# DeltaNet and SwiGLU on one core: weights converted by thirds of columns, the norm's weight moved to x, and a new plan of the start

## The chip, the cores and the metric

The kernel runs on one core of one Trainium2 chip. The metric is the time of one execution in microseconds of device time; the times below are the median of three runs, and one further execution was profiled. Engines are named as in the profile: PE is TensorE (PEld its weight loads), DVE is VectorE, ACT is ScalarE, POOL is GpSimd, and SP issues most of the transfers.

## The reference

Attention first, with a state for each of 4 batches x 8 heads, then a feed-forward network over 3072 tokens. All is float32, except that the kernel gets the three weight matrices as float64 from the host and converts them on the chip.

```
for t in range(768):                                  # q, k, v: (4, 8, 768, 48)
    y[t]  = q[t] @ state                              # k_n = k / (|k| + 1e-6)
    v_old = state.T @ k_n[t]
    state = state + beta[t] * outer(k_n[t], v[t] - v_old)
x   = y as (3072 tokens, 384)
xn  = x / sqrt(mean(x*x) + 1e-6) * rms_g
out = (silu(xn @ w_gate) * (xn @ w_val)) @ w_out      # d_ff = 1536
```

## The kernel before

**Tiling.** The sequence is cut into 12 chunks of 64 steps (`NCH`), each for all 32 heads. Every chunk has the same stages:

- `load` fetches k, q and v. `norms` makes 1/|k|: a square on ACT (L558), a sum on DVE (`ksum`), a power on POOL (`knrm`, L562), then `krec` on DVE.
- `prep` scales k by `krec` (L628), turns it with PE (`turn`, L517), forms the scores k k^T (`scores`, L540), and solves a triangular system: the scores go through DRAM (`dkk`) into a layout by head (`at`, L656). A recursion of fifteen steps on DVE (`step`: L703 and L709) inverts two 32-step blocks at once. The result goes through DRAM again (`dx`) into `mt` and `x2bd`, and PE merges the blocks (L760, L784, L808). For chunks 0 and 1 ("early") DVE does the scaling of `at`; later POOL does.
- `qpart` makes the masked scores of q and k (`pt`, L580).
- `recur` applies the system to v minus the state's part (L895), multiplies with `pt` (L909), updates the state (L1022), takes the mean square (L949 for chunk 0, L961 later), its inverse root (`root`, L966 to L973, on POOL), scales y, and turns it into x for the feed-forward (L990 on PE, L993 copies on ACT).
- The feed-forward of chunks 0 and 1 is `ffn_plain` (L1067 up, L1049 down). From chunk 2 on it is `ffn`, with fewer products from sums of the weights that `factors` and `out_factors` prepare (L1160 up, L1216 down).

**Weights.** `weights` has 18 loads of 768 KB into three `raw` buffers. A load's float64 words become float32 by a Prelu on ACT (L456), two bit operations and one product on DVE (L444, L447, L452), and a sum. The sum is made by PE and ACT for the first three loads (L467, L468, L476), by DVE for the others (L484, L486). For gate and val one load is 128 rows by 768 columns, and the norm's weight g, one number for each row, is multiplied in during the conversion. The list `ready` holds what an up-matmul waits for: all three loads of its matrix and half.

**Order.** Every instruction group goes into the class `Plan` with its engine, an estimated duration and a due time. Plan lays all groups out in time, forward by start time and due time, backward for new due times, 60 rounds with random shakes from a fixed seed, and keeps the best order; this order is then issued, engine by engine. `PERIOD` spaces the due times of the chunks, `STICK` is what a change of PE's tiling mode is charged, `FETCH` and `AHEAD` describe how fast PE can get its instructions and how many it holds, and `after` is the time before which a transfer is not planned. In the planned gaps of PE before 70 us `filler` puts matmuls without a use (L1306). ACT issues some transfers of chunk 0 on a queue of its own; all others go through SP.

Of the kernel before, what the change touches and what calls it, by code (L numbers as in the profile page):

```python
# [18 lines left out]
W = 32  # L19
# [6 lines left out]
STICK = 2.0  # L26
# [23 lines left out]
def fillers(a, b):  # L50

    n, t = 0, max(a, 2.0)
    while t < b - 0.3:
        n, t = n + 1, t + (0.43 if t < 6.5 else 0.24)
    return n


class Plan:
# [47 lines left out]
    def forward(self, banks, until):  # L106
# [13 lines left out]
        while len(order) < len(self.ops):  # L120
            best = None
            for e in ENGINES:
                for op in cand[e]:
                    s = max(op.at, at[e])
                    if op.port:
                        s = max(s, held["POOL" if e == "DVE" else "DVE"])
                    n = sum(not g.taken for g in op.acquire)
                    if n > len(free):
                        continue
                    if n:  # L130
                        s = max(s, free[n - 1])
                    key = op.key + (STICK if op.mode is not None and op.mode != mode else 0.0)
                    if op.size and backlog + op.size - FETCH * op.dur > AHEAD:
                        key += 2.0 * STICK
                    if best is None or (s, key, op.n) < best[0]:
                        best = ((s, key, op.n), op)
# [13 lines left out]
            if op.eng == "PE":  # L150
                if s - at["PE"] > 1.4 and s > until:
                    end += 1.6
                backlog = max(0.0, backlog - FETCH * (s - at["PE"])) + op.size - FETCH * op.dur
                late = max(0.0, backlog - AHEAD) / FETCH
                backlog, end = max(0.0, backlog - FETCH * late), end + late
# [50 lines left out]
    def run(self, free, filler=None, until=0.0):  # L206
# [3 lines left out]
        rng = random.Random(1)  # L210
# [31 lines left out]
def kernel(  # L242
# [46 lines left out]
    g52 = sbt("g52", [128, KT])  # L289
# [72 lines left out]
    PERIOD = 50.5  # L362
# [42 lines left out]
    def load_small():  # L405
        for i in range(8):
            src = beta.rearrange("b (y g) (c i t) -> i g (b y) c t", i=2, g=2, t=W)[i // 2 % 2, i % 2]
            dma(beta_b[16 * i : 16 * i + 16], src, 0.5, w=[("beta", i)], work=0.2)
        dma(g_sb, moe_rms_g.rearrange("(t p) -> p t", p=128), 1, w=["g"], after=8.0)
        P.add("DVE", 0.1, lambda: nc.vector.tensor_scalar_mul(g52, g_sb, 2.0**-52), 30, r=["g"], w=["g52"])  # L410
# [6 lines left out]
    def weights():  # L417
        todo = []
        for half_ in range(2):
            c0 = half_ * WCOL  # L420
            for side, (key, w) in enumerate((("wg", moe_w_gate), ("wv", moe_w_val))):
                for t in range(KT):
                    src = w[t * 128 : t * 128 + 128, c0 : c0 + WCOL]
                    dst = w_in[:, side, half_, 3 * t : 3 * t + 3].rearrange("p i n -> p (i n)")
                    todo.append((dst, src, [(key, half_)], t))
            for f in range(6 * half_, 6 * half_ + 6, 2):
                src = moe_w_out[f * 128 : f * 128 + 256, :].rearrange("(a p) c -> p a c", a=2)
                z = spot(f)
                todo.append((wo_sb[:, z : z + 2].rearrange("p a c -> p (a c)"), src, [("wo", f), ("wo", f + 1)], None))
        for n, (dst, src, keys, gt) in enumerate(todo):  # L430

            gk = [] if gt is None else ["g", "g52"]
            pr = (30 if n < 9 else CV2) + 0.2 * n
            i, a = n % NRAW, n % NCV
            rdst = raw[i] if len(src.shape) == 2 else raw[i].rearrange("p (a c) -> p a c", a=2)
            dma(rdst, src, (0.1 if n == 0 else 3 + 2 * n), w=[("raw", i)], dur=0.7, work=3.06, after=(0.0, 5.0, 16.7, 24.5, 24.5)[n] if n < 5 else 50.0)
            words = raw[i].bitcast(U32).rearrange("p (n two) -> p n two", two=2)
            low, high = words[:, :, 0], words[:, :, 1]
            u = dst.bitcast(U32)
            cc = cvb[a]  # L440
# [10 lines left out]
            def s5(low=low, cc=cc, by=2.0**-52 if gt is None or n < NPE else g52[:, gt : gt + 1]):  # L451
# [7 lines left out]
            P.add("DVE", 1.0, s5, pr, r=[("raw", i)] + gk, w=cvk)  # L459
            done = []  # L460
            if n < NPE:
                for x_ in range(2):
                    ps = Group()
                    cols = slice(384 * x_, 384 * x_ + 384)

                    def s6(ps=ps, dst=dst[:, cols], cc=cc[:, cols]):
                        nc.tensor.matmul(ps.t[:, 0:384], ident, dst, start=True, stop=False)  # L467
                        nc.tensor.matmul(ps.t[:, 0:384], ident, cc, start=False, stop=True)  # L468

                    P.add("PE", 1.35, s6, pr, r=cvk + [("cvw", n), "ident"], w=[("cvp", n, x_)], ps=ps, size=8)  # L470
                    done.append(("cv", n, x_))
                    def s7(dst=dst[:, cols], ps=ps, gt=gt):
                        if gt is None:
                            nc.scalar.copy(dst, ps.t[:, 0:384])
                        else:
                            nc.scalar.mul(dst, ps.t[:, 0:384], g_sb[:, gt : gt + 1])  # L476

                    P.add("ACT", 0.48, s7, pr, r=[("cvp", n, x_), ("cvw", n)] + gk, w=[done[-1]], last=ps)
            else:
                done.append(("cv", n))  # L480

                def s8(dst=dst, cc=cc, gt=gt):
                    if gt is None:
                        nc.vector.tensor_tensor(out=dst, in0=dst, in1=cc, op=ALU.add)  # L484
                    else:
                        nc.vector.scalar_tensor_tensor(out=dst, in0=dst, scalar=g_sb[:, gt : gt + 1], in1=cc, op0=ALU.mult, op1=ALU.add)  # L486

                P.add("DVE", 0.97, s8, pr, r=cvk + gk, w=[("cvw", n), done[-1]])
# [6 lines left out]
    def load(c, what):  # L495
        t0 = c * C
        pk, pq, pv = ((-5, 1, 12), (5, 29, 36))[c] if c < 2 else (due(c, 150), due(c, 99), due(c, 70))
        for key, t, src, pr in (("k2", k2[c % NK], k, pk), ("q2", q2, q, pq)):
            for g in range(2):
# [4 lines left out]
                dma(dst, s, pr, w=[(key, c % NK if key == "k2" else 0, g)], dur=0.7, work=1.02, eng="ACT" if c == 0 and g and key == "k2" else "SP", after=((2.0, 0.0, 26.0), (6.0, 24.5, 34.0))[c]["kqv".index(key[0])] if c < 2 else 60.0)  # L504
        if "v" in what:
            for bb in range(2):
                s = v[2 * bb : 2 * bb + 2, :, t0 : t0 + C, :].rearrange("p h t e -> t (p h) e")
                dma(vt[64 * bb : 64 * bb + 64], s, pv, w=[("v", bb)], dur=0.85, work=1.02, after=(26.0, 34.0)[c] if c < 2 else 60.0)
# [61 lines left out]
    def qpart(c):  # L570
# [3 lines left out]
        turn(q2, qt, qk, [("q2", 0, 0), ("q2", 0, 1), "q2p"], pr, c == 0)  # L574
# [10 lines left out]
    def prep(c):  # L585
# [42 lines left out]
        P.add(e_, 1.1 if early else 1.6, lambda: eng.tensor_tensor(  # L628
            out=kd, in0=kd, in1=krec[i2][:, :, None].to_broadcast([128, 16, D]), op=ALU.mult,
        ), pr if early else pn, r=[("krec", i2)], w=kkeys)  # L630
        turn(kn, kt[ikq], ktk, kkeys + kp, pr, c == 0)
        ps = scores(kt[ikq], kt[ikq], pr, ktk, kkall)
        for d in range(2):
            dst = kk[ikk][:, :, d:16:2]
            src = lambda d=d, ps=ps: ps[d].t.rearrange("p (u i t) -> p i u t", u=8, i=2)
            if c or d == 0:
                P.add("ACT", A(512), lambda dst=dst, f=src: nc.scalar.mul(dst, f(), -1.0), pr, r=[ps[d]], w=kkd(d), last=ps[d])
            else:
                P.add("DVE", V(512), lambda dst=dst, f=src: nc.vector.tensor_scalar_mul(dst, f(), -1.0), pr, r=[ps[d]], w=kkd(d), last=ps[d])
# [55 lines left out]
        P.add(e_, 0.69 if early else 1.3, share1, pi, r=[("at", 0), ("at", 1)], w=xkeys)  # L695
# [35 lines left out]
        q_ = "SP" if c else "ACT"  # L731
        for par in range(2):
            dst = dx[i2].rearrange("i g x (s two) t -> two (i g x) s t", two=2)[par]
            dma(dst, x[64 * par : 64 * par + 64], pi, r=xkeys, w=[("dx", i2, par)], dur=0.63, work=1.0, eng=q_)
# [6 lines left out]
        for i in range(2):  # L741
            for bb in range(2):
                r0 = 64 * bb + W * i
                for g in range(2):
                    src = dx[i2][i, g, 8 * bb : 8 * bb + 8].rearrange("x s t -> s x t")
                    dma(mt[imt][r0 : r0 + W, 8 * g : 8 * g + 8, W * i : W * i + W], src, pi, r=xk, w=[("mt", imt, i, bb, g)])
        for y_ in range(4):
            src = dx[i2][1].rearrange("g (b y) s t -> y s (g b) t", y=4)[y_]
            dst = x2bd[W * y_ : W * y_ + W, :, y_]
            dma(dst, src, pi, r=xk, w=[("x2bd", y_)], eng=q_)  # L750
# [76 lines left out]
    def recur(c):  # L827
# [115 lines left out]
        for h in halves:  # L943
# [21 lines left out]

            def root(cols=cols):  # L966
                m = ms[i2][:, cols, 0]
                if c == 0:
                    nc.gpsimd.tensor_tensor(out=m, in0=m, in1=ms[i2][:, cols, 1], op=ALU.add)
                nc.gpsimd.tensor_scalar_add(m, m, 1e-6)  # L970
                nc.gpsimd.tensor_tensor(out=rs[i2][:, cols], in0=m, in1=mhalf[:, cols], op=ALU.pow)

            P.add("POOL", 1.1, root, py, r=["half"], w=[(k_, i2, p) for p in h for k_ in ("ms", "rs")])  # L973
# [11 lines left out]
            for p in h:  # L985
                psx = Group()

                def xtr(p=p, psx=psx):
# [4 lines left out]
                P.add("ACT", A(384), lambda p=p, psx=psx: nc.scalar.copy(  # L993
                    xdst[:, p:6:2], psx.t[:, 0:DM].rearrange("d (k t) -> d k t", k=KT)
                ), pxv, r=[psx], w=[xkeys[p]], last=psx)
# [15 lines left out]
        if c < NCH - 1:  # L1011
# [15 lines left out]
            for g in range(2):  # L1027
# [4 lines left out]
                else:  # L1032
                    P.add("DVE", V(384), lambda dst=dst, f=src: nc.vector.tensor_copy(out=dst, in_=f()), py + 3, r=[pss[g], ("xp", 0), ("xp", 1)], w=[("st", g)], last=pss[g])
# [22 lines left out]
    def ffn_plain(c, f0, f1, start):  # L1056
# [3 lines left out]
        def up(f):  # L1060
            ps = Group()
            h_, i_, n = f // 6, f % 6 // 2, 128 * (f % 2)
            for side, key in enumerate(("wg", "wv")):
# [8 lines left out]
                P.add("PE", 1.31, mm, start + 3.9 * (f - f0), r=xk + [("wuse", h_)] + ready[(key, h_)], w=[ps, (("sil", f % 2), ("hf", f, 0))[side]], ps=ps, size=12)  # L1072
# [40 lines left out]
    def factors(h):  # L1113
# [3 lines left out]
        wk = ready[("wg", h)] + ready[("wv", h)]  # L1117
# [80 lines left out]
    def down(c, start):  # L1198
# [12 lines left out]
        x, y, z_ = Group(), Group(), Group()  # L1211

# [28 lines left out]
        product(x, s2, s2k, wsum[:, 1], False, 4)  # L1241
        snap(u2, x, [("tmp", 0)])
# [9 lines left out]
        product(x, a(1, 1), ak(1, 1), wsum[:, 2], False, 12)  # L1252
        P.add("ACT", A(192), lambda: nc.scalar.copy(o_sb[1][:, 0:192], x.t[:, 0:192]), -1, r=[x], w=[("tmp", 4)], last=x)
# [86 lines left out]
```

## Time and profile before

| what | value |
|---|---|
| median of 3 runs (lowest to highest) | 721.37 us (721.09 to 725.16) |
| the profiled execution: time, span | 720.97 us, 718.9 us |
| busy share of the span: PE, PEld, DVE, ACT, POOL | 98%, 91%, 76%, 42%, 22% |
| first feed-forward matmul (L1067) | 75.43 us |
| fillers (L1306) | 320 records, 42.6 us |
| up-matmuls from chunk 2 on (L1160) | 2400 records, 305.4 us |
| moved by DMA | 54.68 MB, mean 76 GB/s |

The profile is of one execution. A matmul in float32 has two records. Matmuls are pipelined and their ends are modelled, so a busy PE is not PE at its peak. "issue" is time in which an engine waited for nothing that the profile shows. The chain of work that ended last is followed back from the last instruction, at each step to what released it, or to the instruction before it on its engine. A rate of the DMA over a stretch is the mean over all its queues.

### The profile page before, as it was taken

Reading aid. Unit: us, or ns where it says so; the run is one execution under the profiler, and the core shown is the slowest. Engines: PE = TensorE matmul, PEld = TensorE weight load, DVE = VectorE, ACT = ScalarE, POOL = GpSimd, SP = SyncE. Lnnn points to the kernel's source line nnn. Section 1 sums busy time; section 2 is a strip of 40 time slices with the busy share of each in tenths; the row PEclk is TensorE's granted clock in tenths of the full one; section 3 lists DMA queues with packets and bytes.
Section 4 is the critical chain, followed back from the end, with each engine's and each line's share of the span. In section 5 each row is a group of like instructions: output and inputs, shape, how many; then the busy total and the mean of one; then the engine's idle time right before and its main releaser. Section 6 shows DMA issues by size and latency. Waiting matters only on the chain.

```text
span 718.9 us, 23523 instructions
## 1 busy us (share of the span) xinstructions
PE 704.4 (98%) x10200; PEld 656.6 (91%) x10200; DVE 549.5 (76%) x1132; ACT 302.8 (42%) x679; POOL 155.3 (22%) x153
## 2 busy tenths in 40 slices
PE   8997998999999999999999999999999999999997
PEld 8796886877789999999999999999999999999997
DVE  5999789798979859829958959769669768648372
ACT  5423553324334535344435534445344445254240
POOL 4102207015132132122132132134032031000000
PEclk9999999999999999999999999999999999999999
DMA  8848688151262251351262352432521442100000
GB/s 184 217 73 219 174 205 232 21 96 25 46 118 47 35 108 25 56 107 25 45 121 46 48 95 47 79 64 46 90 53 26 79 64 38 24 18 2 23 1 23
DMA packets 206999, 54.68 MB, mean 76 GB/s; under 512 B 199216, under 2 KB 202288, under 8 KB 206896
## 3 DMA queue, kind: packets, MB, share of 16 engines
q1 hardware_dynamic: 201552, 52.19, 35.8%
q10 hardware_dynamic: 5344, 0.98, 0.8%
q8 instruction: 80, 1.31, 0.8%
q14 instruction: 23, 0.19, 0.1%
HBM read 40.83 MB, written 12.32 MB: 74 GB/s over the span
## 4 chain that ended last, share of the span: by engine, by line
PE 88%; DVE 7%; DMA 2%; issue 1%; SPq 1%; POOL 1%; ACT 0%; DVEq 0%; ACTq 0%
PE bank L1160 37%; PE bank L1216 19%; PE bank L1067 9%; PE bank L1049 4%; PE bank L849 3%; PE bank L540 3%; PE bank L517 2%; PE bank L895 2%; PE bank L808 2%; PE bank L909 2%; DVE acc L709 2%; PE bank L1022 1%; DVE acc L703 1%; PE bank L990 1%; PE bank L784 1%
## 5 line engine op out<-in xcount | busy, mean ns | idle before, releaser
L1160 PE MATMUL bank<-xf,w_in 128*128 128x128 f32 x1440 | 180.7, 277 | 0.0
L1170 DVE TENSOR_TENSOR tmp<-tmp,bank 128x512 f32<-128x512 f32 x180 | 121.4, 683 | 72.0 <-PE bank L1160 66.0
L1160 PEld LDWEIGHTS bank<-xf,w_in 128*128 128x128 f32 x1440 | 169.9, 192 | 2.4 <-issue 0.4
L1160 PE MATMUL bank<-xf,more 128*128 128x128 f32 x960 | 124.7, 277 | 0.0
L1160 PEld LDWEIGHTS bank<-xf,more 128*128 128x128 f32 x960 | 115.7, 192 | 1.7 <-issue 0.6
L1172 ACT COPY tmp<-bank 128x512 f32<-128x512 f32 x120 | 69.1, 586 | 73.2 <-PE bank L1160 56.9
L1176 ACT ACTIVATE tmp<-tmp 128x256 f32<-128x256 f32 x120 | 49.8, 418 | 100.0 <-DVE tmp L1170 99.9
L709 DVE TENSOR_REDUCE acc<-acc 128x30 f32<-128x90 f32 (+4 forms) x180 | 85.1, 473 | 6.2
L703 DVE TENSOR_TENSOR acc<-acc,at 128x60 f32<-128x60 f32 (+4 forms) x180 | 62.5, 347 | 5.2 <-POOL at L686 2.1
L1216 PE MATMUL bank<-wo_sb,hf 128*128 128x192 f32 x360 | 64.1, 328 | 0.2 <-DVE pt L580 0.2
L1216 PEld LDWEIGHTS bank<-wo_sb,hf 128*128 128x128 f32 x360 | 58.2, 190 | 0.7 <-DVE pt L580 0.4
L1177 DVE TENSOR_TENSOR hf<-tmp 128x256 f32<-128x256 f32 x120 | 52.9, 451 | 5.7 <-ACT tmp L1176 5.1
L562 POOL TENSOR_TENSOR knrm<-ksum,half 128x16 f32<-128x16 f32 x12 | 36.3, 3026 | 92.9 <-DVE ksum L561 87.8
L656 POOL TENSOR_TENSOR at<-at,beta_b 128x1024 f32<-128x1024 f32 x10 | 24.4, 2440 | 131.5 <-DMA at<-dkk 98.6
L1306 PE MATMUL bank<-ident 128*128 128x128 f32 x320 | 42.6, 294 | 1.4 <-POOL ident masks.py:199 1.4
L1306 PEld LDWEIGHTS bank<-ident 128*128 128x128 f32 x320 | 40.5, 207 | 2.4 <-POOL ident masks.py:199 1.4
L730 POOL COPY acc<-acc 128x128 f32<-128x128 f32 x40 | 21.1, 556 | 82.0 <-DVE acc L709 81.8
L1049 PE MATMUL bank<-wo_sb,hf 128*128 128x384 f32 x96 | 34.9, 492 | 0.0
L1225 DVE TENSOR_TENSOR tmp<-tmp,bank 128x192 f32<-128x192 f32 x30 | 10.6, 352 | 31.4 <-PE bank L1216 29.7
L1067 PE MATMUL bank<-xf,w_in 128*128 128x256 f32 x144 | 33.6, 384 | 0.0
L1067 PE MATMUL bank<-xp,w_in 128*128 128x256 f32 x144 | 33.5, 382 | 0.0
L1067 PEld LDWEIGHTS bank<-xf,w_in 128*128 128x128 f32 x144 | 27.1, 192 | 4.8 <-issue 0.4
(167 smaller groups left out, 1052.8 us busy)
## 6 DMA issues: line engine op xcount, KB each, us to landing
at<-dkk SPq DMA_DIRECT2D x23, 256.0 KB, 4.2
more<-in_moe_w_gate_dram SPq DMA_DIRECT2D x6, 768.0 KB, 4.7
q<-in_q_dram SPq DMA_DIRECT2D x24, 192.0 KB, 3.8
more<-in_moe_w_val_dram SPq DMA_DIRECT2D x6, 768.0 KB, 7.6
vt<-in_v_dram SPq DMA_DIRECT2D x24, 192.0 KB, 4.3
more<-in_moe_w_out_dram SPq DMA_DIRECT2D x6, 768.0 KB, 7.3
out_dram<-tmp SPq DMA_DIRECT2D x48, 96.0 KB, 2.2
k<-in_k_dram SPq DMA_DIRECT2D x23, 192.0 KB, 3.6
```

Of the source, the lines that this page charges most:

```text
L562: P.add("POOL", 2.95, lambda: nc.gpsimd.tensor_tensor(out=knrm[i2], in0=ksum[i2], in1=half, op=ALU.pow), pn, r=[("ksum", i2), "half"], w=[ ...
L703: nc.vector.tensor_tensor(out=acc[:, 1:3, 0:n, j + 2 : W].rearrange("p a i t -> p i a t"), in0=acc[:, old, 0:n, j : j + 2, None].to_broadc ...
L709: nc.vector.tensor_reduce(out=acc[:, new, 0:n, j + 2 : W], in_=acc[:, lo : lo + 3, 0:n, j + 2 : W].rearrange("p a i t -> p i t a"), axis=A ...
L1049: nc.tensor.matmul(po[p].t[:, 0:DM], hf[:, spot(f), 128 * p : 128 * p + 128], wo_sb[:, spot(f)], start=(f == f0), stop=(f == f1 - 1), skip ...
L1067: nc.tensor.matmul(ps.t[:, TOK * side : TOK * side + TOK], w_in[:, side, h_, 3 * t + i_, n : n + 128], x_[:, 2 * t : 2 * t + 2].rearrange( ...
L1160: nc.tensor.matmul(g.t[:, 128 * z : 128 * z + 128], fac[:, side, 128 * f : 128 * f + 128], xf[:, xs], start=(begin and z == 0), stop=False ...
L1170: P.add("DVE", V(512), lambda t=t, g=g: nc.vector.tensor_tensor(out=t, in0=t, in1=g.t, op=ALU.add), -1, r=[g], w=[tk], last=g)
L1172: P.add("ACT", A(512), lambda t=t, g=g: nc.scalar.copy(t, g.t), -1, r=[g], w=[tk], last=g)
L1176: P.add("ACT", A(256), lambda t=t: nc.scalar.activation(out=t[:, 0:256], in_=t[:, 0:256], func=ACTF.Silu), -1, w=[tk])
L1177: P.add("DVE", V(256), lambda t=t, f0=f0, p=p: nc.vector.tensor_tensor(out=hf[:, spot(f0) : spot(f0) + 2, 128 * p : 128 * p + 128], in0=t[ ...
L1216: nc.tensor.matmul(g.t[:, 0:192], a_[:, f], b_[:, f], start=(begin and f == 0), stop=(f == 5), skip_group_check=True)
L1306: nc.tensor.matmul(warm[:, 0:128], ident, ident)
```

## The change

Line numbers in the profile of the changed kernel differ by a few from those before. The parts:

- Gate and val are loaded and converted by 256 columns and all 384 rows, not by 128 rows and 768 columns. The order of the loads alternates gate and val, with w_out's among them; `ready` is kept by third, and an up-matmul waits for its own third.
- g is no longer multiplied into the weights. It is applied when x is copied out of PSUM: three scaled copies of 128 columns for each half of the tokens in place of one copy of 384.
- The transfers of chunk 0 that carry the solved blocks alternate between the ACT and SP queues.
- For chunk 0's root, DVE adds the two partial sums and 1e-6 in one instruction; POOL keeps the power.
- Some copies of chunks 0 and 1 move from DVE to ACT; the scaling of chunk 1's k moves from DVE to POOL; the first copy of the state moves from DVE to ACT.
- In the last chunk one product of the down-projection gets a PSUM bank of its own and comes earlier; its result is added at the end.
- Plan: until 130 us fetches are taken as slower and fewer instructions as held; the mode charge, the seed, `PERIOD`, the fillers' spacing and the planned times of the first transfers have new values.

```diff
-STICK = 2.0
+EARLY, FETCH0, AHEAD0 = 130.0, 42.0, 130.0
+STICK = 1.0
...
-        n, t = n + 1, t + (0.43 if t < 6.5 else 0.24)
+        n, t = n + 1, t + (0.43 if t < 6.5 else 0.26)
...
-                    if op.size and backlog + op.size - FETCH * op.dur > AHEAD:
+                    rate, store = (FETCH, AHEAD) if s > EARLY else (FETCH0, AHEAD0)
+                    if op.size and backlog + op.size - rate * op.dur > store:
                         key += 2.0 * STICK
...
+                fill = 17.0 if s < until else 0.0
+                backlog = max(0.0, backlog - (rate - fill) * (s - at["PE"])) + op.size - rate * op.dur
+                late = max(0.0, backlog - store) / rate
...
-        rng = random.Random(1)
+        rng = random.Random(19)
...
-    PERIOD = 50.5
+    PERIOD = 51.0
...
-                for t in range(KT):
-                    src = w[t * 128 : t * 128 + 128, c0 : c0 + WCOL]
-                    dst = w_in[:, side, half_, 3 * t : 3 * t + 3].rearrange("p i n -> p (i n)")
-                    todo.append((dst, src, [(key, half_)], t))
+            for i_ in range(3):
+                for side, (key, w) in enumerate((("wg", moe_w_gate), ("wv", moe_w_val))):
+                    c1 = c0 + 256 * i_
+                    src = w.rearrange("(t p) c -> p t c", p=128)[:, :, c1 : c1 + 256]
+                    todo.append((w_in[:, side, half_, i_:9:3], src, [(key, half_, i_)]))
...
-            dma(rdst, src, (0.1 if n == 0 else 3 + 2 * n), w=[("raw", i)], dur=0.7, work=3.06, after=(0.0, 5.0, 16.7, 24.5, 24.5)[n] if n < 5 else 50.0)
+            dma(rdst, src, (0.1 if n == 0 else 3 + 2 * n), w=[("raw", i)], dur=0.7, work=3.06, after=(0.8, 5.0, 16.7, 24.5, 24.5, 33.3, 50.0)[n] if n < 7 else 53.0)
...
-            def s5(low=low, cc=cc, by=2.0**-52 if gt is None or n < NPE else g52[:, gt : gt + 1]):
+            def s5(low=low, cc=cc, by=2.0**-52):
...
-                    cols = slice(384 * x_, 384 * x_ + 384)
+                    cut = slice(2 * x_, 2 + x_)
+                    m = 512 - 256 * x_
...
-        turn(q2, qt, qk, [("q2", 0, 0), ("q2", 0, 1), "q2p"], pr, c == 0)
+        turn(q2, qt, qk, [("q2", 0, 0), ("q2", 0, 1), "q2p"], pr, False)
...
-        P.add(e_, 1.1 if early else 1.6, lambda: eng.tensor_tensor(
+        en, n_ = (nc.gpsimd, "POOL") if c else (nc.vector, "DVE")
+        P.add(n_, 1.6 if c else 1.1, lambda: en.tensor_tensor(
...
-        q_ = "SP" if c else "ACT"
+        turns = itertools.cycle(("SP",) if c else ("ACT", "SP"))
...
-            dma(dst, x[64 * par : 64 * par + 64], pi, r=xkeys, w=[("dx", i2, par)], dur=0.63, work=1.0, eng=q_)
+            dma(dst, x[64 * par : 64 * par + 64], pi, r=xkeys, w=[("dx", i2, par)], dur=0.63, work=1.0, eng=next(turns))
...
+            def mean(cols=cols):
+                nc.vector.scalar_tensor_tensor(
+                    out=ms[i2][:, cols, 0], in0=ms[i2][:, cols, 0], scalar=1e-6, in1=ms[i2][:, cols, 1], op0=ALU.add, op1=ALU.add
+                )
...
-                if c == 0:
-                    nc.gpsimd.tensor_tensor(out=m, in0=m, in1=ms[i2][:, cols, 1], op=ALU.add)
-                nc.gpsimd.tensor_scalar_add(m, m, 1e-6)
+                if c:
+                    nc.gpsimd.tensor_scalar_add(ms[i2][:, cols, 0], ms[i2][:, cols, 0], 1e-6)
...
-                P.add("ACT", A(384), lambda p=p, psx=psx: nc.scalar.copy(
-                    xdst[:, p:6:2], psx.t[:, 0:DM].rearrange("d (k t) -> d k t", k=KT)
-                ), pxv, r=[psx], w=[xkeys[p]], last=psx)
+                for k_ in range(KT):
+                    P.add("ACT", A(128), lambda p=p, psx=psx, k_=k_: nc.scalar.mul(
+                        xdst[:, 2 * k_ + p], psx.t[:, 128 * k_ : 128 * k_ + 128], g_sb[:, k_ : k_ + 1]
+                    ), pxv, r=[psx, "g"], w=[xkeys[p]], last=psx)
...
-                P.add("PE", 1.31, mm, start + 3.9 * (f - f0), r=xk + [("wuse", h_)] + ready[(key, h_)], ...
+                P.add("PE", 1.31, mm, start + 3.9 * (f - f0), r=xk + [("wuse", h_)] + ready[(key, h_, i_)], ...
...
+        if c == NCH - 1:
+            v_ = Group()
+            product(v_, a(1, 1), ak(1, 1), wsum[:, 2], True, 3)
+            snap(p4, v_, ["xc", ("xp", 0), ("xp", 1)])
...
-        product(x, a(1, 1), ak(1, 1), wsum[:, 2], False, 12)
-        P.add("ACT", A(192), lambda: nc.scalar.copy(o_sb[1][:, 0:192], x.t[:, 0:192]), -1, r=[x], w=[("tmp", 4)], last=x)
+        if c == NCH - 1:
+            add(1, 0, p4, x, ["xc"])
+        else:
+            product(x, a(1, 1), ak(1, 1), wsum[:, 2], False, 12)
+            P.add("ACT", A(192), lambda: nc.scalar.copy(o_sb[1][:, 0:192], x.t[:, 0:192]), -1, r=[x], w=[("tmp", 4)], last=x)
```

## The prediction

> **What bounds the kernel now.** I read the page first, then the busy time of each engine by stage, then the chain that ended last, then the timeline of the three places the chain points to. By stage (columns: stretch, length, busy time of PE, PEld, DVE, ACT and POOL, PE clock, DMA share, GB/s):
>
> ```profile
> 0.00:75.43 75.43, 68.61 (x1023) 61.76 (x1023) 61.39 (x130) 32.61 (x67) 15.39 (x21) 0.96 0.74 177
> ...
> 100.00:110.00 10.00, 9.14 (x226) 7.05 (x221) 9.61 (x17) 6.11 (x12) 0.00 (x0) 1.00 1.07 256
> 110.00:115.00 5.00, 4.00 (x125) 2.78 (x123) 4.86 (x9) 3.11 (x7) 4.40 (x4) 1.00 1.08 260
> 115.00:121.00 6.00, 4.96 (x89) 4.53 (x90) 5.93 (x4) 1.94 (x4) 5.84 (x5) 0.72 0.55 155
> ...
> 300.00:600.00 300.00, 300.00 (x4687) 291.19 (x4686) 227.82 (x501) 136.43 (x313) 73.16 (x70) 1.00 0.36 64
> ```
>
> From 121 us on PE is never idle until the last product: the time from there is the sum of PE's own work. Only three places can give time: the start-up before the first feed-forward matmul (75.43 us), the stalls between 100 and 121 us, and the tail. In the start-up PE looks busy, but 42.6 us of it are fillers (L1306); the chain there runs over DVE, ACT and POOL (columns: start, us, what):
>
> ```profile
> 25.78 1.23 DVE at L656
> ...
> 56.98 0.32 DVE m1bd L773
> ...
> 66.89 0.20 POOL ms L969
> ...
> 67.18 0.51 POOL ms L970
> ...
> 67.76 0.86 POOL rs L971
> 68.62 1.00 POOL ms L969
> ...
> 69.70 1.43 POOL ms L970
> ...
> 71.20 0.59 POOL rs L971
> ...
> 75.64 5.36 PE bank L1067 x24
> ...
> 114.00 2.04 issue
> ...
> 119.28 1.52 PE bank L849 x64
> ```
>
> See that the root sums hold the chain from 66.89 to 71.79 us, and that at 114 PE waits 2.04 us for nothing shown. Three rows of the timeline give the transfers and the tail:
>
> ```profile
> 48.36 3.88 SPq L359 DMA_DIRECT2D mt<-dx  x8
> ...
> 56.89 0.84 DVE L773 COPY m1bd<-bank 32x256 f32<-32x256 f32 x2
> ...
> 712.54 2.22 PE L1216 MATMUL bank<-wsum,hf 128*128 128x192 f32 x12 [0.45 <-DVE tmp L1225]
> ```
>
> [...] The queue is in this trace (q8, 80 packets, 1.31 MB: 16 KB each)[...]: with DMA at 1.07 to 1.08 PE lost 0.86 us at 108.16 and 2.04 at 114.00. [...] eight mt transfers take 3.88 us of issue on SP. [...] Here six L1067 matmuls take 1.29 us, and 1.49 after a 64-row group: 0.2 per return.
>
> **The change, part by part.** I place each step on the start-up chain with durations of before and the order of instructions of the changed kernel as built.
>
> *k behind q.* SP now issues both halves of q before its half of k. k was issued at 2.83 us and landed at 6.40. Its issue comes at 0.79 + 2 x 0.76 = 2.3, but 393 KB of q goes ahead, 2.0 us at the 199 GB/s of the first 20 us, part of it in engine time that was idle. I take +0.5; bounds -0.5 and +1.5. So the first krec is ready at 13.46 instead of 12.96.
>
> *DVE until the first block recursion.* Taken off DVE: two copies of kt and qt (0.68 each), kk (0.68), the second k scaling (0.96, now POOL, 1.5) and g52 (0.16): 3.16 us. But the gain is not free to appear. In the new order DVE does two masks (1.29), k scaling (0.95), a conversion step (0.95), one of 0.56, bk 0.18, and only then the second ksum (0.95 + 0.17), so it ends near 18.5; the POOL power takes 3.03, to 21.6, and krec (0.43), two masks (1.28), POOL's scaling holding the next step a little (0.3) and the third conversion (2.07) follow: L656 at 25.7 against 25.78. POOL's power is late next; the removal is worth 0 here (0 to -0.8). What ACT takes over, four copies of 0.59, lies in time when ACT is half idle (9.17 of 20 us busy in 20 to 40).
>
> *First chunk's transfers on two queues.* The recursion still ends near 42.3. Before, dx was issued on ACT at 43.99 and 44.59, behind a 1.04 us zero fill, and landed by 48.36. Now the spread is followed at once by dx, one half on each queue: about 42.9 and 43.2, landed near 47.0. The four mt transfers that the transpose needs then take two issue slots on each queue, 1 us. Fillers (88 x 0.228 = 20.1 us from 30.6) end at 50.7: the transpose L760 moves from 52.36 to 50.7. That alone would be hidden, for before its result lay until DVE came to it at 56.89. In the new order this copy stands after four steps of chunk 1's recursion, not six (two pairs, 1.94 us): 54.95.
>
> *To the root.* Merges and fillers follow as before, with five fillers where six were; the first L895 moves from 63.20 to 60.9. L909 now comes in two halves without fillers ahead; the last square of ACT moves from 67.35 to 65.1, a Prelu of 0.93 standing between the halves.
>
> *Root sums on DVE.* Before: 0.20 + 0.51 + 0.86 + 1.00 + 1.43 + 0.59 and gaps, 4.9 us on POOL in series. Now two DVE sums (0.17 each by the L561 row, hidden between recursion steps, but each can wait 0.7 for the step in front) and two powers (0.86, 0.59). The last rs: 66.6 instead of 71.79.
>
> *g on x.* Each xf copy becomes three with a scale from a tile. 192 columns take 319 ns, 384 take 482, so 128 would be 265; a scale from a tile adds 0.1 (384 columns: 582 against 482). Running back to back I take 0.31, six are 1.9 us against 0.95, and the square of the next k (0.85) and a spread (0.74) now stand among them on ACT: from the last scaling (67.5) to the first L1067 4.3 us instead of 2.9. First L1067 at 71.8 instead of 75.43: **-3.6** (bounds -5.4 and -1.5). From chunk 2 on the longer copy path is hidden: at 511.66 the copies start, the sums end at 514.99, and L1160 needs them only at 519.09.
>
> *Conversion by thirds.* The same 18 loads, four to six passes each. The first four groups of up-matmuls now need two converted tiles and not all six. Before, the last of them was ready at 70.6, 4.8 us ahead of need; in the new order tile after tile comes ahead of need too, with 71.8 (tiles of the third pair near 71 and 78, used near 88). Worth 0; without it the earlier start would have been lost.
>
> *Late instruction fetches.* The stalls cost 0.86 + 2.04 idle, and 1.35 us of slow clock after (L849 1.52 for 1.08, L990 1.28 for 0.82, L517 0.45 more): 4.25 us. Before, from 98.65 to 116 seven groups of small matmuls stand among 6.5 us of large ones; in the new order eight of them stand among some 11 us. Against that, DMA must still carry the second half's weights. I take **-2.7**; bounds -4.25 and 0.
>
> *Tail.* The last product no longer waits for the sum in front of it: **-0.45**.
>
> *Mode changes.* Small groups stand in 87 runs instead of 84: 3 x 0.2 = **+0.6** (0 to +1.0).
>
> Sum: -3.6 - 2.7 - 0.45 + 0.6 = -6.15. The profiled execution took 720.97 us (span 718.9 and 2.07 around it), so 714.8; the median of the runs is 0.4 above it: **715.2**.
>
> **The rivals.**
> 1. All that the parts offer: start -5.4 (k not late, ACT's copies short) and no stall: -5.4 - 4.25 - 0.45 + 0.3 = -9.8, 711.6 us. For it: most of the start's gain is already there at rs. Against: DMA still runs full near 100 us.
> 2. The order doesn't hide the fetches, or k's delay eats the start: stalls stay at 4.25, -3.45, 717.9; or start -1.5 with stalls halved, 717.8. For it: no transfer is removed, and they are only laid elsewhere.
> 3. Slower: fetch stalls multiply. The feed-forward starts earlier while the same weights are still to load, so PE asks for blocks when DMA is fullest, between 72 and 125 us. Each stall costs 2.1 us with its slow clock (4.25 for two). What else is gained is 3.45, so it decides from two more stalls; with six in all, +8.5 - 3.45: 726.4. Against: the new order spreads the small groups.
>
> **How the numbers follow.** Forecast 0.45, rival 1 0.22, rival 2 0.26, rival 3 0.07. This kernel's measurement tells about 1% (7.2 us) from no change: 714.2 and 728.6. Below 714.2 lie rival 1 and two fifths of the forecast: 0.40; above 728.6 a part of rival 3: 0.03. The range leaves out the outer part of rivals 1 and 3: 711 to 720.
>
> **What would show it.** First L1067 near 71.8 (right if 70 to 74); L656 near 25.7; POOL's two powers alone after the squares, rs near 66.6; the m1bd copy near 55; idle PE in 75 to 130 under 2 us; no gap ahead of the last product. The prediction is wrong if PE shows "issue" waits of several us there, if PE idles at the start of a later feed-forward, or if k lands after 8 us.

## The result, and the profile after

The changed kernel takes 720.5 us (median of 20 runs, 718.19 to 721.93) against 721.96 us for the kernel before (20 runs beside it, 718.23 to 725.16). The ratio is 0.9977, with a 95% interval of 0.9963 to 0.9992: faster by 0.2%, where 0.9% was forecast, and outside the range on the slow side. The two profiled executions have the same span, 719.0 against 718.9 us.

First the stages of the changed kernel (columns: stretch, length, busy time of PE, PEld, DVE, ACT and POOL with their instructions, PE clock, DMA share, GB/s):

```profile
0.00:75.43 75.43, 67.29 (x1005) 60.22 (x1006) 59.50 (x125) 35.12 (x76) 14.54 (x19) 0.93 0.74 168
...
100.00:110.00 10.00, 10.00 (x218) 7.42 (x217) 9.76 (x16) 5.47 (x12) 0.14 (x1) 1.00 0.87 223
110.00:115.00 5.00, 4.42 (x142) 3.26 (x141) 4.93 (x8) 4.09 (x12) 3.67 (x3) 1.00 1.01 260
115.00:121.00 6.00, 5.41 (x77) 4.53 (x76) 5.86 (x7) 3.32 (x6) 5.23 (x3) 1.00 0.89 194
121.00:130.00 9.00, 7.57 (x60) 5.76 (x53) 8.79 (x15) 2.55 (x5) 4.79 (x4) 1.00 0.45 122
300.00:600.00 300.00, 298.39 (x4728) 288.97 (x4728) 228.87 (x491) 141.19 (x332) 72.76 (x74) 1.00 0.36 64
```

See two things. Between 75 and 130 PE still loses 3.1 us, only in other places: 0.58 in 110 to 115, 0.59 in 115 to 121, 1.43 in 121 to 130 and 0.51 before. And the stretch from 300 to 600, where PE was never idle before, has lost 1.6 us. PE's waits, the page's list (columns: line and what it waited for, us in total, times, longest), say what for:

```profile
PE bank L840 <- issue: 1.4, 1, 1.4
...
PE bank L509 <- DVE hf L1072: 1.2, 1, 1.2
PE bank L509 <- issue: 0.6, 1, 0.6
PE bank L986 <- ACT yn L980: 0.6, 1, 0.6
PE bank L532 <- issue: 0.5, 1, 0.5
```

"Issue" is a wait for nothing shown. Of it only 1.1 us are left between 75 and 130, where 2.9 were; 2.0 us of waits for VectorE and ACT have come in their place (0.27 for r not shown here), and 1.4 us of issue stand later, in chunk 5.

What an "issue" wait of PE is, the traces can tell. They hold the transfers of a queue that the page calls "instruction" (q8: 80 packets, 1.31 MB, so blocks of 16 KB). In the 14 profiled executions PE has 33 such waits, and every one ends 1.2 to 1.7 us after a block has landed: those of the kernel before at 108.16 and 114.00 end 1.3 and 1.6 us after it, the one at L840 above 1.3 us. The reading is that PE waits there for instructions. Five later ones that are put down to a conversion on ACT (L460 in e3, e5, e6 and e7, L456 in e9) end in the same way; the waits for L1072, L980 and L854 in this list don't. Now the chain of the start-up (columns: start, us, what):

```profile
2.56 5.02 DMA k<-in_k_dram
...
18.63 5.40 DMA more<-in_moe_w_gate_dram
24.06 0.91 ACT w_in L460
24.99 0.70 DVE w_in L448
25.72 0.96 DVE tmp L451
26.70 0.62 DVE tmp L456
27.58 1.23 DVE at L646
...
57.56 0.32 DVE m1bd L764
...
64.29 0.68 PE bank L886 x32
```

SP's half of the first k lands near 7.6 us instead of 6.4. The first recursion (L646, L656 before) starts at 27.58 instead of 25.78, behind the third weight load and its conversion. L451, one of the two bit passes, takes 0.96 us where it (L447) took 0.56. By the first feed-forward matmul 1.8 us of delay have turned into a gain, but one of 0.9 us only:

```profile
74.54 4.05 PE L1064 MATMUL bank<-xf,w_in 128*128 128x256 f32 x18
```

From there to the end of the span the changed kernel takes 644.5 us and the kernel before took 643.5 (718.9 - 75.43). PE's idle time up to its last product grew from 3.5 to 5.0 us; its busy time fell from 635.8 to 635.3, although 1.35 us of slow clock, which the execution before showed between 115 and 121 (0.72, now 1.00), are absent.

### The profile page after: what moved, and what is told of

It reads as the page before. It is cut to its first block, busy times and chain, and to the rows that moved or that the text cites. A ratio compares the mean times of both kernels' runs of the same rounds, so it can differ in the third digit from the quotient of the medians.

```text
span 719.0 us, 23540 instructions
## 1 busy us (share of the span) xinstructions
PE 701.6 (98%) x10178; PEld 652.8 (91%) x10178; DVE 553.8 (77%) x1128; ACT 314.3 (44%) x732; POOL 152.1 (21%) x150
## 3 DMA queue, kind: packets, MB, share of 16 engines
q8 instruction: 80, 1.31, 0.8%
## 4 chain that ended last, share of the span: by engine, by line
PE 79%; DVE 12%; DMA 4%; issue 2%; SPq 1%; POOL 1%; ACT 1%; ACTq 0%; DVEq 0%; POOLq 0%
PE bank L1157 36%; PE bank L1214 19%; PE bank L1064 6%; PE bank L1046 3%; PE bank L532 3%; PE bank L840 2%; PE bank L509 2%; DVE acc L699 2%; DMA more<-in_moe_w_gate_dram 2%; PE bank L799 2%; PE bank L886 1%; PE bank L1019 1%; PE bank L900 1%; DVE w_in L480 1%; DVE acc L693 1%
## 5 line engine op out<-in xcount | busy, mean ns | idle before, releaser
L646 POOL TENSOR_TENSOR at<-at,beta_b 128x1024 f32<-128x1024 f32 x10 | 25.6, 2555 | 146.1 <-DMA at<-dkk 146.1
L720 POOL COPY acc<-acc 128x128 f32<-128x128 f32 x40 | 17.1, 458 | 116.9 <-DVE acc L699 116.1
L1312 PE MATMUL bank<-ident 128*128 128x128 f32 x298 | 40.3, 296 | 1.4 <-POOL ident masks.py:199 1.4
L1312 PEld LDWEIGHTS bank<-ident 128*128 128x128 f32 x298 | 38.1, 209 | 2.5 <-POOL ident masks.py:199 1.4
L1046 PE MATMUL bank<-wo_sb,hf 128*128 128x384 f32 x96 | 34.3, 491 | 0.3 <-DVE r L854 0.3
L1064 PE MATMUL bank<-xf,w_in 128*128 128x256 f32 x144 | 33.6, 382 | 0.0
L1064 PE MATMUL bank<-xp,w_in 128*128 128x256 f32 x144 | 33.4, 383 | 0.0
L1064 PEld LDWEIGHTS bank<-xf,w_in 128*128 128x128 f32 x144 | 26.8, 190 | 4.9
L1064 PEld LDWEIGHTS bank<-xp,w_in 128*128 128x128 f32 x144 | 26.7, 190 | 4.4 <-issue 0.2
```

Of the source, the lines that this page charges most:

```text
L1046: nc.tensor.matmul(po[p].t[:, 0:DM], hf[:, spot(f), 128 * p : 128 * p + 128], wo_sb[:, spot(f)], start=(f == f0), stop=(f == f1 - 1), skip ...
L1064: nc.tensor.matmul(ps.t[:, TOK * side : TOK * side + TOK], w_in[:, side, h_, 3 * t + i_, n : n + 128], x_[:, 2 * t : 2 * t + 2].rearrange( ...
L1312: nc.tensor.matmul(warm[:, 0:128], ident, ident)
```

## The experiments

Two theories stood against each other. *Placement*: the parts work as reckoned, but two of them have a price that was not seen, the passes over thirds and the place of k in SP's queue, and both fall on the start. *Limits behind*: whatever the start gains, the stretch from 75 to 130 gives back, because instruction fetches, weights or VectorE hold PE there. Ratios are of the kernel before run beside each; with 14 to 22 runs an interval is some 0.2% to either side, with 4 to 12 runs 0.2 to 0.4%. Start times in a single execution scatter: four kernels whose start-up is the same but for POOL's sums (e2, e5, e11, e12) have their first L1064 at 71.89, 71.11, 70.75 and 71.66.

**e1: thirds side by side.**

```diff
-todo.append((w_in[:, side, half_, i_:9:3], src, ...))
+todo.append((w_in[:, side, half_, 3 * i_ : 3 * i_ + 3], src, ...))
 # readers: slot 3*t + i_ becomes 3*i_ + t
```

> The changed kernel, with each converted third of w_in side by side in memory (256 x 3 columns in one piece) and every reader of w_in remapped; the order of all instructions is that of the changed kernel. Theory A (the two bit passes of a gate or val load, L448 and L451, take 0.69 and 0.95 us instead of 0.55 and 0.56 only because they write or read three separate pieces): L448 0.55, L451 0.56, L460 unchanged at about 0.85; each of the 12 loads costs 0.5 us less on VectorE, 6 us in all. Three of these passes lie on the start-up chain before L646 and three before the second L646, so L646 moves from 27.58 to about 27.0 and the first L1064 from 74.43 to 73.3 or so; VectorE, which is full between 75 and 130, gives back waits of PE there: end 2 to 3 us earlier, 716.5 to 718.5. Rival B (the passes are slow because the loads come as three pieces or because other engines use the memory at the same time): L448 and L451 stay, time unchanged within 0.5 us. Rival C (passes faster, but what holds PE between 75 and 130 is the arrival of weights): VectorE 5 to 6 us less busy, first L1064 about 1 us earlier, end within 1 us of the changed kernel.

Measured: 719.97 us, ratio 0.999 (0.997 to 1.0011); first L1064 at 73.76. L451 by tile (columns: tiles, count, shortest, median and longest in ns, first and last start), first of the changed kernel, then of e1:

```profile
L451 DVE TENSOR_SCALAR more<-w_in x6: 943/950/954, 19.3 to 143.2; 128x768 uint32<-128x768 uint32 x6
```

```profile
L451 DVE TENSOR_SCALAR more<-w_in x6: 550/556/561, 18.7 to 144.3; 128x768 uint32<-128x768 uint32 x6
```

The scattered thirds are the whole cause of the slow passes: L451 falls to 0.56 us, L448 from 0.68 to 0.55, and VectorE is busy 548.4 us instead of 553.8. In the changed kernel L451 reads three pieces and writes one run of 768, and L448 works in place on three pieces; on w_out's weights, one piece in both kernels, L451 takes 0.56 us in both. Why three pieces cost L451 more (0.39 us) than L448 (0.13), no run shows. The end, in which the saving should show, doesn't show it. PE's waits for VectorE are gone, but PE comes to L509 sooner than in the changed kernel (112.21 instead of 114.57), and the block of instructions that lands ahead of the wait's end moves later (113.67 instead of 112.96): PE stands 3.25 us at 116.11. That is Rival C in form, with instructions in place of weights. On top comes the slow clock, which is back in this execution, with a mean of 0.83 from 110 to 130 us (1.00 in e2):

```profile
116.92 6.37 PE L1064 MATMUL bank<-xp,w_in 128*128 128x256 f32 x18
```

At a clock of 1.00 the same 18 records take 4.05 us (e2, at 114.91). A slow clock stands here in the profiled executions of the kernel before (0.72 from 115 to 121), e1, e4 and e12 (0.91 each from 110 to 130), after waits of 2.0 to 3.3 us; e2, e9 and e11 wait 2.8 to 3.3 us and don't have it (1.00 from 90 to 130). What decides it stays open, and so does how much of e1's missing gain is its doing.

**e2: e1, and k first.** SP issues its half of the first k before both halves of q; nothing else moves.

```diff
-SP: q, q, k, w_gate, ...
+SP: k, q, q, w_gate, ...
```

> The kernel of contiguous thirds, and SP issues its half of the first k before the two halves of the first q; nothing else moves. If the q halves ahead of k cost the start what the changed profile suggests (k landed at 7.6 instead of 6.4): k lands at 6.4 and the first square of k starts at 6.5; the first krec comes 1.2 us earlier. If that delay is carried to the end of the start-up, the first L1064 is another 1.2 us earlier than with contiguous thirds alone, and the end too. Rival: the third weight load (landed at 24.06) and the transfer of at (landed near 27.4) hold L646 and don't depend on k: L646 stays within 0.4 us of the run with contiguous thirds, and so does the end.

Measured: 718.29 us, ratio 0.9973 (0.9956 to 0.999). The first square of k starts at 5.21 us instead of 7.64 in e1. In PE's timeline:

```profile
71.89 4.05 PE L1064 MATMUL bank<-xf,w_in 128*128 128x256 f32 x18
```

L646 starts at 25.77, 1.6 us earlier than in e1, and the first L1064 1.9 us. So the rival falls: the third weight load held L646 here too, but it is issued behind dkk, which waits for k, and moves with it (issued at 16.92 instead of 18.51). With both prices taken away the start gains 3.5 us on the kernel before, and the median is 3.1 us below it. PE's wait at L509 stays at 3.3 us.

**e3 and e4: the root sums.** e3 is the changed kernel with the sums back on POOL, e4 the kernel before with only this edit.

```diff
 # e3 (e4: the reverse)
-nc.vector.scalar_tensor_tensor(out=m, in0=m, scalar=1e-6, in1=ms[..., 1], op0=add, op1=add)
+nc.gpsimd.tensor_tensor(out=m, in0=m, in1=ms[..., 1], op=add)
+nc.gpsimd.tensor_scalar_add(m, m, 1e-6)
```

> The changed kernel with the sum in front of the first chunk's two roots back on POOL (sum, add, power for each half, six POOL instructions instead of two); the rest of the order is the same. Theory A (the root stretch is on the start-up chain and what it costs is carried to the end): POOL takes 4.9 us from the last square to rs instead of 1.5 to 1.8, the first L1064 moves from 74.43 to about 77.5 and the end 3 us later than the changed kernel, about 723.5. Rival (start-up gains are eaten between 75 and 130, where VectorE and the weights are late anyway): the first L1064 is 3 us later but the end less than 1 us later.

> The kernel before with one edit: the sum in front of the first chunk's two roots in one VectorE instruction each, as in the changed kernel, so that POOL has two powers left; the order of everything else is that of the kernel before. POOL's stretch shrinks from 4.9 to about 1.6 us if VectorE reaches the two sums at once; each can stand up to 1 us behind a recursion step. Theory A (what the start gains reaches the end): first L1067 at 72.0 to 73.0 instead of 75.43, end 2.5 to 3.3 us earlier, 718.5 against 721.5. Rival (the stretch from 75 to 130 gives it back, because there the fetch stalls and the weights don't move): first L1067 earlier as said, end within 1 us of the kernel before.

Measured: e3 719.29 us, ratio 0.9976 (0.9954 to 0.9998), first L1064 at 74.29; e4 719.41 us, ratio 0.9977 (0.9956 to 0.9998), first L1067 at 74.02. POOL in e3's timeline:

```profile
68.33 0.20 POOL L963 TENSOR_TENSOR ms<-ms 128x1 f32<-128x1 f32 x1
...
68.61 0.29 POOL L964 TENSOR_SCALAR ms<-ms 128x1 f32<-128x1 f32 x1
...
68.99 0.58 POOL L965 TENSOR_TENSOR rs<-ms,mhalf 128x1 f32<-128x1 f32 x1
```

Both theories of e3 fall at their first step. POOL's second root takes 1.2 us there, and rs is done at 69.57, earlier than with VectorE's sums (70.14), which stand behind recursion steps. The two sums, 0.20 and 0.29 us here, took 1.01 and 1.42 us in the kernel before, while conversion passes of VectorE (L452 at 68.55, L486 at 69.59) ran beside them. In the new order these passes come after 71.3. That the passes slow POOL is a reading of these two executions; no run moves the passes alone. The edit gains 1.4 us of start in the old order, less than the 2.4 to 3.4 that both theories of e4 had, and nothing in the new one. e4's end moves by 2.0 us, with an interval of 0.1 to 3.2: it fits Theory A better, and does not exclude the rival.

**e6 and e7: g on x, and the two queues,** both from the changed kernel.

```diff
 # e6
-for k_ in range(KT): nc.scalar.mul(xdst[:, 2 * k_ + p], psx.t[...], g_sb[:, k_ : k_ + 1])
+nc.scalar.copy(xdst[:, p:6:2], psx.t[:, 0:DM]...)
 # e7: dx and x2bd on ACT, mt on SP, as before
```

> The changed kernel, but each group of three scaled copies of xf is one plain copy of 384 columns, and g is left out of the computation. In the changed kernel the six copies take 0.30 us each, 1.8 us on ACT ahead of the first L1064 where two copies would take 0.95. Theory A (they are on the start-up chain): the first L1064 comes 0.4 to 0.9 us earlier, 73.6 to 74.1, and the end by as much, since the twelve fillers that stand in front of L1064 in PE's order end at 74.5 and take part of it. Rival (fillers hold L1064, and later copies are hidden): first L1064 within 0.2 us, end unchanged within what 3 rounds can tell.

> The changed kernel with the first chunk's transfers on the queues of the kernel before: both dx and the four x2bd on ACT, the eight mt on SP; the order of all other work stays. Theory A (the two queues bring the transposition forward, as the prediction said): L751 starts 1 to 2 us later than 53.4, but DVE's m1bd copy at 57.5 stands behind four recursion steps and PE waits 2.9 us for it, so that the first L1064 moves by less than 0.3 us: the two queues are worth nothing here. Rival (they are on the chain): the first L1064 at 75.3 or later, the end 1 us later.

Measured: e6 719.24 us, ratio 0.9978 (0.9963 to 0.9993), first L1064 at 74.74; e7 719.04 us, ratio 0.9971 (0.9955 to 0.9987), first L1064 at 74.92. Neither differs from the changed kernel. In e7 the transposition L751 starts at 54.23 instead of 53.41, but 0.74 of these 0.82 us stand already at L646 (28.32 instead of 27.58), ahead of the edit: the two queues don't bring even this step forward. PE waits 2.46 us for VectorE's m1bd copy behind it. So the two queues are worth nothing here, and the six copies are hidden.

**e5: half of the bytes,** from e2.

```diff
-dma(rdst, src, ...)
+dma(rdst[:, :, half_w], src[:, :, half_w], ...)   # half of the columns for loads 9 to 17
```

> The kernel of contiguous thirds with k first, but the nine weight loads of the second half bring only the left half of each row, so that 3.5 MB less cross the DMA queues between about 75 and 120 us; everything that is issued and computed stays, on weights that are partly not those of the reference. In that kernel PE stood 3.3 us still at L509 (114.5) with nothing shown that it waits for, and 0.9 us at L840 (332). Theory F (PE waits for instructions, and their transfers are held up by the weight loads): the wait at 114.5 falls below 1 us and the end comes 2 to 3.5 us sooner than with contiguous thirds and k first; the 0.9 us at 332, where DMA is little used, stay. Rival G (PE has used up what is fetched ahead because several groups of small matmuls follow each other, whatever DMA does): both waits stay within 0.5 us and the end too.

Measured: 716.5 us, ratio 0.9926 (0.9899 to 0.9953). PE's waits, e2 first, then e5:

```profile
PE bank L509 <- issue: 3.3, 1, 3.3
...
PE bank L840 <- issue: 0.9, 1, 0.9
```

```profile
PE bank L509 <- DVE hf L1072: 1.6, 1, 1.6
...
PE bank L840 <- issue: 1.1, 1, 1.1
...
PE bank L509 <- ACT w_in L460: 0.7, 1, 0.7
```

The last of these lines is a wait for instructions too. In PE's timeline, e2 first, then e5:

```profile
114.48 0.60 PE L509 MATMUL bank<-ident,q 128*128 128x128 f32 x4 [3.32 <-issue]
```

```profile
110.68 0.60 PE L509 MATMUL bank<-ident,q 128*128 128x128 f32 x4 [0.68 <-ACT w_in L460]
```

It is the same group of matmuls, L460 on w_in had ended at 109.96, before the wait began, and the wait ends 1.3 us after a block has landed (108.40 to 109.36; in e2 111.78 to 112.91, 1.6 us before the end). So with the DMA share between 90 and 110 at 0.70 instead of 1.01 the wait falls from 3.3 to 0.7 us, as Theory F had it. One execution each, but e1, e2, e11 and e12 have the same order there and all of the bytes, and wait 2.8 to 3.3. The one at L840 at 332 us stays (DMA share 0.36 from 300 to 600 in the changed kernel). So the wait near 115 is for instructions, as far as these runs show, and it grows with the bytes of the weight loads (0.7 us with half of them in nine loads, 2.8 to 3.3 with all). The transfer of a block is not what grows (1.0 us in e5, 1.1 in e2): it starts later, 1.3 us after PE has begun the L509 group ahead of the wait in e2, 1.0 us before in e5. When it was asked for, the trace doesn't tell. But 1.8 us of waits for VectorE come up in its place (1.55 and 0.27), with a slow clock behind the second (8 records of L1046 in 4.54 us, 2.75 in e2; mean clock 0.91 from 110 to 130), and the end is 1.8 us sooner where 2 to 3.5 were expected. Two limits of almost the same height lie over each other there.

**e11: products between small groups,** from e2.

```diff
-chunk 5: L886 x64, L840 x64, product, L900 x64, product
+chunk 5: L886 x64, product, L840 x64, product, L900 x64
```

> The kernel of contiguous thirds with k first; in chunk 5 one product of the feed-forward (four large matmuls) is put between the two groups of 64 small ones, L886 and L840, that follow each other at 330, and one between L840 and L900 where one stood before; nothing else moves. Theory F2 (126 small matmuls in a row use up the fetched instructions, and that is the 0.9 us at L840): the wait goes or falls below 0.3 us, and what is behind it comes 0.6 to 0.9 us sooner, less 0.2 for one more return from the 64-row form: the end 0.5 us sooner, which the runs can hardly tell. Rival (the wait stands at a fixed place in the program, where a block of instructions ends): the wait is found again, within 1 us of the same place, of the same size.

Measured: 716.93 us, ratio 0.9931 (0.9901 to 0.9961, 8 runs). In PE's timeline the wait is gone:

```profile
328.49 1.16 PE L1157 MATMUL bank<-xf,more 128*128 128x128 f32 x8
329.57 1.46 PE L840 MATMUL bank<-state,qt 64*64 64x48 f32 x64
```

L840 takes 1.46 us instead of 1.15, so 0.6 us is gained. From the first product of chunk 2 to the last one of the kernel idle PE falls from 0.90 to 0.07. So two groups of 64 records of small matmuls in a row were what PE waited behind, though the DMA share is low there (0.42 from 320 to 336 in the changed kernel); e2's wait, too, ends 1.3 us after a block. The median is 1.4 us below that of e2, but the intervals overlap, as was expected for half a microsecond.

**e8, e9, e10: operations and planner.** e8 is the changed kernel with one fetch rate; e9 its operations with the whole planner of before; e10 the operations of before with the changed planner.

```diff
 # e8
-rate, store = (FETCH, AHEAD) if s > EARLY else (FETCH0, AHEAD0)
+rate, store = (FETCH, AHEAD)
 # e9 also: STICK = 2.0, random.Random(1), fillers of 0.24; e10: the reverse of e9 in the kernel before
```

> The changed kernel planned with one rate of instruction fetch for the whole time, as the kernel before was, so that the order of all engines is another one with the same work. Theory A (the plan that knows of late fetches spreads the small groups between 90 and 120): PE's unexplained waits between 75 and 130 grow from 1.1 us to 3 to 5 us, and the end is 1.5 to 3 us later than the changed kernel. Rival (the fetch terms bring nothing, since what is spared in waits for instructions is waited for VectorE): waits for instructions and for VectorE together stay at 3 to 3.5 us between 75 and 130, and the end is within 1 us of the changed kernel.

> The changed kernel's operations, laid out by the planner of the kernel before (one rate of instruction fetch, STICK 2.0, seed 1, fillers of 0.24 us): what the code changes do without the planner's. Theory A (the planner's part carries the change: the same operations under one fetch rate and the new seed gave 731.1): slower than the kernel before, 723 to 732, with over 3 us of unexplained waits of PE before 125 us. Rival (731.1 was a bad draw of that one plan, and the operations alone are worth what the whole change is): 719 to 721.5.

> The operations of the kernel before, laid out by the changed planner (two fetch rates, STICK 1.0, seed 19): what the planner's part does alone. Theory A (the planner's part spares waits for instructions, whatever is planned): unexplained waits of PE between 75 and 130 below 1.5 us instead of 2.9, and 717 to 720. Rival (an order fits only the operations that it was made for, and each plan is a draw): waits of 2.5 us or more there, 721 to 730.

Measured: e8 731.06 us (1.0133, 1.0096 to 1.0171), e9 727.08 us (1.0081, 1.0051 to 1.011), e10 727.37 us (1.0083, 1.0059 to 1.0106). e8 has 3.7 us of issue at L532 (80.32), before its first L1064 at 84.7. Theory A of e8 has the direction, but the loss of 10 us is far above its 1.5 to 3. e9 waits 5.7 us between 90 and 130, all of it for instructions. e10 does spare issue there (0.5 us at L853 is left), but its first L1071 comes at 78.24, behind waits for ACT's yn and xf, and 727 is the price. Neither half of the change gains alone: 721.5 for both old, 727.1 and 727.4 for the mixtures, 720.5 for both new. This is what e10's rival said, that an order is a draw that fits the operations it was made for: the three other draws came out 6 to 10 us slower. Three draws don't show what the fetch terms are worth on the average.

**e12: together.** e11, with the root sums on POOL and chunk 4's k loaded behind chunk 3's v.

> All that the runs so far point to, together: contiguous thirds, k first, the products between the small groups of chunk 5, the root sums back on POOL, and the loads of chunk 4's k (0.39 MB, issued at 107 to 108.6 in front of the place where PE waits for instructions) moved behind chunk 3's v at 125. Theory: the wait of 3.3 us at L509 falls to 2 to 2.7, since less stands in the DMA queues at 107 to 114, and waits for VectorE of 1 to 2 us remain behind it, as with half of the bytes; the first L1064 at 71.5 to 71.9; 716.5 to 718, that is 0.993 to 0.996 of the kernel before. Rival (the wait is kept by the weights alone, and k's loads come late for their use): the wait at L509 stays at 3.2 or more, and the end is that of contiguous thirds with k first, 718.3, or later.

Measured: 717.43 us, ratio 0.9947 (0.9926 to 0.9967). The wait at L509 stays at 3.06 us, nearer to the rival's 3.2 than to the 2 to 2.7 of the theory, so taking 0.39 MB of k out of the queue is too little. The time lies where the theory put it, but it is that of e11 within the intervals, and the profiled execution has 1.4 us of slow clock behind the wait. e11 has the lowest median of the versions that compute the whole result, 0.7% below the kernel before; the runs can't tell it from e12.

## Why the prediction was wrong

- *k behind q* (+0.5 on the landing): the direction was right, the size off, though inside its bounds. k landed 1.2 us later, and undoing it (e2) gives 1.9 us at the first L1064.
- *DVE until the first block recursion* (25.7): it failed. Measured 27.58. POOL's power was named as late next; late was the third weight load, issued at 18.63 instead of 16.21. SP's queue was followed for k alone, not for what stands behind dkk, which waits for k. Of the 2.7 us by which the first feed-forward matmul missed its forecast (74.54, not 71.8), 1.9 stand here.
- *Conversion by thirds, "worth 0", "the same 18 loads, four to six passes each"*: it failed. The count was right, the durations were carried over to another access pattern: +0.13 us for L448 and +0.39 for L451, twelve times each, where g's leaving gives back 0.06 each for nine passes of L456 and nine of L480. Undoing the pattern (e1) moves the first L1064 by 0.8 us, which is no more than such start times scatter.
- *Two queues*: from L646 to the m1bd copy 29.9 us pass, 31.1 before and 29.25 in the forecast. Two thirds of the forecast came, and not from the queues: with the old ones it is 29.9 too (e7). That leaves the new order, as the forecast had it; no run takes the order alone away.
- *Root*: from the last square to rs 1.9 us, 1.5 forecast. Size right, cause wrong: in the new order POOL's sums are short without the move (0.20 and 0.29 us in e3); in the old one the move gains 1.4 us (e4).
- *g on x*: 3.6 us from the last scaling to the first L1064, 4.3 forecast. Hidden (e6).
- *Start, -3.6*: -0.9. With the two mis-sized prices out, -3.5 (e2).
- *Late fetches, -2.7*: it failed, and not at the fetches. Their cost fell from 4.25 us to 1.1, by more than was forecast: waits from 2.9 to 1.1, and no slow clock. But 2.0 us of waits for VectorE and ACT came, so that idle PE went from 2.9 to 3.1 us. The forecast put at nothing what else limits this stretch. VectorE is full there (9.76, 4.93 and 5.86 us busy of 10, 5 and 6), it was so before (the rows in the prediction: 9.61, 4.86 and 5.93), and what one limit spares the other takes (e1, e5). That the slow clock was absent was hoped for, and is luck as far as the runs show: it is back in e1, e5 and e12 (mean clock 0.83, 0.91 and 0.91 from 110 to 130).
- *Tail, -0.45*: right, no gap stands ahead of the last product at 712.62.
- *Mode changes, +0.6*: right in size. Busy PE after the start is 0.8 us longer once the slow clock is taken off; that mode changes are the cause, no run shows.
- *Not in the sum*: 1.4 us at L840 in chunk 5 (e11). The new order was read between 75 and 130, not behind. Nor is PE quite without a wait after 121 us in the kernel before: 0.2 us at 244.

In the profiled executions the terms measure -0.9 (start), -1.1 (fetches, with what came in their place), -0.45, +0.8 and +1.6 (L840, and 0.2 beside it): nothing in sum, as the spans say. The medians of 20 runs differ by 1.5 us.

Rival 2 was the nearest: "k's delay eats the start" and the stalls stay. It ended at 717.9 because it let one of the two happen, where both came, with the wait at L840 on top.

## What to carry to other kernels

When a change cuts the same work differently, price each pass by its new access pattern, and not by the row of the old one (L451: 0.95 us for 0.56). Where an order is planned, follow every queue behind the instruction that is moved, and look for runs of small instructions in the whole program, not only where the stalls were (1.4 us at L840). And before counting a stall as gained, see how full the next engine is in just that stretch.

## What the hardware showed that was not expected

Instructions came late, and with more data in transfer they came later. All 33 waits of PE for nothing shown, in 14 profiled executions, end 1.2 to 1.7 us after a 16 KB block of instructions has landed. With the same order of work PE stood 2.8 to 3.3 us at one place in four executions (DMA share between 90 and 110 from 0.99 to 1.05), and 0.7 us with half the bytes of nine weight loads (0.70). Two of POOL's smallest operations, 0.20 and 0.29 us in e3, took 1.01 and 1.42 us in the kernel before beside conversion passes of VectorE (L452, L486); in the other direction a pass of VectorE (L480) took 3.00 us for 0.96 in the changed kernel while POOL scaled at (L646, 117.13 to 120.30).
